# A second MLP's first layers in block products: seven products of half blocks in place of eight, with the sums of the weights made ahead

## Chip, core and metric

One core of one Trainium2 chip runs the whole program in one launch. The metric is the device time of the launch in microseconds, the median of several runs. TensorE is called PE here, VectorE DVE, ScalarE ACT, GpSimd POOL, and SyncE, whose queue issues the transfers, SP.

## The reference

Attention with its softmax on the queries (over the head's 64 numbers) and on the keys (over the sequence) gives 4608 tokens of 512 numbers. They go through two pairs of layers:

```python
# attention: q_s, k_s = softmaxes of q (last axis) and k (axis 2)
kv = np.einsum('bhsd,bhse->bhde', k_s, v)
x = np.einsum('bhsd,bhde->bhse', q_s, kv)      # 8 x 8 heads, 576 x 64
# then as 4608 x 512:
h = x @ w_in                                   # 512 x 2048
x = np.maximum(0.01 * h, h) @ w_out            # 2048 x 512
h = np.maximum(np.maximum(x @ w1, x @ w2), x @ w3)   # each 512 x 768
out = h @ w_out2                               # 768 x 512
```

All is float32 outside; the weights reach the chip as 64-bit words.

## The kernel before

The tokens stand in nine chunks of N = 512. Every operand of a product is kept as a high and a low part, and one product of blocks is three matmuls into one PSUM bank (`mm3`): high by high, high by low, low by high. A matmul has 128 rows, 128 columns of weights and 512 tokens. Two pools hold four banks each: `ps` for first layers, `ps_acc` (tile `acc`) for last layers.

The first pair (stage A) works through the chunks in the turns of the table TURNS, 16 steps of a block of 128 hidden numbers each. In a step PE makes the first layer's block (`project`, 12 matmuls), ACT takes it from the bank, ACT and DVE split it (`split_g`), and PE then makes the last layer's part of the step before (`a_out`, 12 matmuls). Beside it run units of background work, one stage per step: the attention of later chunks (`kv_unit`, `q_unit`) and, from step 33 on, the preparation of the second pair's weights. Each of 24 `ahead_unit`s loads 512 KB of raw words, splits them (`split_words`) into high and low parts in a buffer `room` of the pool `wp` and stores these to a DRAM tile `wb`. The results of stage A are stored to DRAM tiles `x2`.

In stage B the 12 prepared blocks of 1 MB (`weights_ready`, L170) stay in `wp`, which has 17 buffers of 1 MB. For each chunk and each of six m (MB = 6 blocks of 128 hidden numbers) three `project`s of 12 matmuls are made; ACT copies the first bank (L596), DVE takes the maximum with the second and the third (L597, L598), `split_g` makes the two parts, and PE makes the last layer's part of the m before (`b_out`, 12 matmuls). After the last m of a chunk ACT and DVE in turn copy four banks to `st` (L440, L438), and SP stores them (L441).

Each engine works its instructions off in its own order and waits for the others by semaphores. A scheduler puts the instructions of an engine in order when the program is built; the source decides it but for small shifts.

## Time and profile before

| | |
|---|---|
| runs | 1474.90, 1474.41, 1474.42 us; median 1474.42 |
| profiled execution (the span of its profile) | 1474.5 us |
| PE busy | 1455.5 us, 6984 matmuls |
| weight loads on PE | 1199.1 us, beside the matmuls |
| DVE busy | 730.3 us |
| ACT busy | 491.4 us |
| transfers | 129.24 MB |

Busy times are sums over instructions of the profiled execution. Matmuls follow each other before the one ahead has ended, so the mean length of one (390 ns) is more than the time from one to the next. Every DMA of the kernel is issued by SP.

### The profile page before, as it was taken

How to read it: one execution, taken by the hardware profiler on the slowest of the kernel's cores; microseconds unless marked ns; L12 is line 12 of the kernel's file. 1: busy time of each engine (PE TensorE's matmuls, PEld its weight loads, DVE VectorE, ACT ScalarE, POOL GpSimd, SP SyncE). 2: the span in 40 equal slices, each digit the busy share in tenths (PEclk: the TensorE clock that was granted, in tenths of full speed). 3: DMA queues.
4: the chain of work that ended last, by engine and by line, in shares of the span. 5: the costliest groups of instructions: out<-in, count | busy, mean ns of one | idle time of the engine just before them, and what ended most of it. 6: DMA issues, size and time to landing. Idle time of an engine off the chain costs nothing.

```text
span 1474.5 us, 17669 instructions
## 1 busy us (share of the span) xinstructions
PE 1455.5 (99%) x6984; PEld 1199.1 (81%) x6984; DVE 730.3 (50%) x1386; ACT 491.4 (33%) x968; POOL 28.6 (2%) x42
## 2 busy tenths in 40 slices
PE   7999999999999999999999999999999999999998
PEld 5688878888888888888888888888888888888887
DVE  9779955867666676765662162213122222222222
ACT  6755853444344344433432231212111111112111
POOL 0000100000000000000000000000000000000000
PEclk9999999999999999999999999999999999999999
DMA  9235532314232231412205580101010100000000
GB/s 356 85 116 185 205 98 72 107 62 130 72 125 78 85 129 62 129 57 68 93 30 186 199 338 33 58 1 58 0 58 3 56 29 29 29 0 29 1 29 29
DMA packets 45203, 129.24 MB, mean 88 GB/s; under 512 B 4672, under 2 KB 4672, under 8 KB 39488
## 3 DMA queue, kind: packets, MB, share of 16 engines
q1 hardware_dynamic: 45120, 128.11, 25.2%
q8 instruction: 55, 0.90, 0.3%
q14 instruction: 28, 0.23, 0.0%
HBM read 89.29 MB, written 38.80 MB: 87 GB/s over the span
## 4 chain that ended last, share of the span: by engine, by line
PE 96%; DVE 2%; ACT 1%; DMA 0%; issue 0%; SPq 0%; ACTq 0%
PE ps L410 56%; PE acc L410 37%; PE ps L377 1%; PE ps L258 1%; DMA spare<-in_q_dram 0%; DVE spare L344 0%; DVE nmx L224 0%; DVE qmx L325 0%; PE ps L359 0%; DVE spare L335 0%; DVE qsm L338 0%; DVE ca L130 0%; DVE raw L133 0%; DVE ca L134 0%; ACT spare L236 0%
## 5 line engine op out<-in xcount | busy, mean ns | idle before, releaser
L410 PE MATMUL ps<-xhi,w 128*128 128x512 f32 x2448 | 777.1, 390 | 1.9 <-DVE xlo L394 1.2
L410 PEld LDWEIGHTS ps<-xhi,w 128*128 128x128 f32 x2448 | 460.2, 188 | 98.6 <-DVE xlo L394 1.5
L410 PE MATMUL ps<-xlo,w 128*128 128x512 f32 x1224 | 476.6, 390 | 0.0
L410 PE MATMUL acc<-ghi,w 128*128 128x512 f32 x1152 | 381.9, 393 | 0.0
L410 PEld LDWEIGHTS ps<-xlo,w 128*128 128x128 f32 x1224 | 230.2, 188 | 48.2 <-ACT xlo L391 0.3
L410 PEld LDWEIGHTS acc<-ghi,w 128*128 128x128 f32 x1152 | 216.0, 188 | 46.6 <-ACT ghi L430 0.2
L431 DVE TENSOR_TENSOR glo<-g,ghi 128x512 fp32r<-128x512 f32 (+1 forms) x201 | 136.2, 679 | 227.7 <-ACT ghi L430 227.7
L410 PE MATMUL acc<-glo,w 128*128 128x512 f32 x576 | 224.5, 390 | 0.3 <-DVE glo L431 0.3
L430 ACT ACTIVATE ghi<-g 128x512 fp32r<-128x512 f32 (+1 forms) x201 | 125.2, 625 | 216.3 <-DVE g L598 208.8
L597 DVE TENSOR_TENSOR g<-g,ps 128x512 f32<-128x512 f32 x54 | 37.2, 688 | 306.1 <-PE ps L410 306.1
L552 ACT ACTIVATE g<-ps 128x512 f32<-128x512 f32 x144 | 85.5, 595 | 258.8 <-PE ps L410 255.5
L410 PE MATMUL acc<-w,ghi 128*128 128x512 f32 x432 | 132.8, 389 | 0.0
L410 PEld LDWEIGHTS acc<-glo,w 128*128 128x128 f32 x576 | 108.2, 188 | 22.3 <-DVE glo L431 0.5
L596 ACT ACTIVATE g<-ps 128x512 f32<-128x512 f32 x54 | 32.4, 599 | 201.1 <-PE ps L410 201.1
L410 PEld LDWEIGHTS acc<-w,ghi 128*128 128x128 f32 x432 | 81.0, 188 | 16.8
L598 DVE TENSOR_TENSOR g<-g,ps 128x512 f32<-128x512 f32 x54 | 37.2, 688 | 106.0 <-PE ps L410 106.0
L410 PE MATMUL acc<-w,glo 128*128 128x512 f32 x216 | 83.9, 389 | 0.0
L440 ACT ACTIVATE st<-acc 128x512 f32<-128x512 f32 x68 | 38.5, 599 | 60.4 <-PE acc L410 60.2
L410 PEld LDWEIGHTS acc<-w,glo 128*128 128x128 f32 x216 | 40.6, 188 | 8.5
L249 POOL PARTITION_ALL_REDUCE mx<-mx x24 | 25.5, 1063 | 629.2 <-DVE mx L248 619.1
L131 ACT ACTIVATE room<-ca 128x512 fp32r<-128x512 f32 x24 | 15.2, 633 | 56.0 <-DVE ca L130 56.0
L534 ACT ACTIVATE xhi<-xf 128x512 fp32r<-128x512 f32 x36 | 20.0, 623 | 36.9 <-PE ps L410 33.5
(110 smaller groups left out, 941.1 us busy)
## 6 DMA issues: line engine op xcount, KB each, us to landing
raw<-in_wa_dram SPq DMA_DIRECT2D x16, 1024.0 KB, 7.8
x<-st SPq DMA_DIRECT2D x64, 256.0 KB, 3.4
room<-in_wb_dram SPq DMA_DIRECT2D x24, 512.0 KB, 3.9
wb<-room SPq DMA_DIRECT2D x24, 512.0 KB, 3.0
w<-wb SPq DMA_DIRECT2D x12, 1024.0 KB, 5.1
xf<-x SPq DMA_DIRECT2D x9, 1024.0 KB, 4.9
out_dram<-st SPq DMA_DIRECT2D x36, 256.0 KB, 2.1
vt<-in_v_dram SPq DMA_DIRECT2D x24, 325.0 KB, 4.1
```

What stands on the lines that cost most here:

```text
L131: nc.scalar.activation(hi, af, AF.Copy)
L249: nc.gpsimd.partition_all_reduce(mx, mx, P, bass_isa.ReduceOp.max)
L258: nc.tensor.matmul(acc[z, : D + 1], lhsT=ke[:, r, z], rhs=vt[:, r, h], start=r == 0, stop=r == RK - 1)
L410: nc.tensor.matmul(acc, lhsT=l, rhs=r, start=first and i == 0, stop=last and i == 2)
L430: nc.scalar.activation(hi[:, z], g[:, z], AF.Copy)
L431: nc.vector.tensor_tensor(lo[:, z], g[:, z], hi[:, z].bitcast(F32), op=ALU.subtract)
L440: nc.scalar.activation(st, acc, AF.Copy)
L534: nc.scalar.activation(hi[:, kk], xf[:, kk], AF.Copy)
L552: nc.scalar.activation(g, acc, AF.Prelu, alpha=0.01)
L596: nc.scalar.activation(g, accs3[0], AF.Copy)
L597: nc.vector.tensor_tensor(g, g, accs3[1], op=ALU.max)
L598: nc.vector.tensor_tensor(g, g, accs3[2], op=ALU.max)
```

## The change

Chunk 0 of the second pair is computed as before. Chunks 1 to 8 are taken two by two. The tokens of a pair are put into two sides of 512 (the first halves of both chunks, the second halves), so that with the 512 inputs in two halves and two m's of weights at a time a product of 2 x 2 blocks arises. It is made by Strassen's seven block products in Winograd's form. A unit (t, j) is the pair of m's t and the first layer j; there are nine units in a pair of chunks, of seven products of six matmuls (L798). Of the weights' half blocks a11, a12 and a22 are operands themselves, and with a21 they make the four sums s1 to s4, which are the other four operands; the tokens' side has one operand to each of the seven (`operands`, named after the weights' operand that it meets).

A bank collects several products, and its sum on the way is read out by ACT (`snap`, L818) before the next product is added. `out` makes the four results of a unit from snapshots and banks (L829, L833: sums on DVE; L827: a copy on ACT) and keeps the maximum over j (L835). With j = 2 it makes the two parts of h (L842 on ACT, L843 on DVE). The last layers take the left side of tokens in `out_left` (24 matmuls for each t), the right side in `out_right` (18 for each block of 128 rows); they stand between s1 and s3 of some iterations as `fill`.

The sums of the weights are made in stage A by nine `ahead_unit`s, which store them to a DRAM tile `stream` in the order of use, and the plain halves to `plainw` for chunk 0. In the pair part they are loaded as groups of four products, 1 MB each, three groups ahead (`load_group`, 65 times). Tokens of a chunk are stored as two halves per piece throughout, so that the rows of the output go out by `store_rows`, 48 transfers in place of 36, copied from the bank by ACT alone.

```diff
+PAIRS = ((1, 2), (3, 4), (5, 6), (7, 8))
+H = N // 2
+USES = ("a11", "a12", "a22", "s2", "s4", "s1", "s3")
+LATE = ("a22", "s4")
+PARTS = ("a21", "a11", "a12", "a22", "s2", "s4", "s1", "s3")
...
-    ready = [[dp.tile([P, 2, 2, N], F32, name=f"wb{m}{i}") for i in range(2)] for m in range(MB)]
-
-    def ahead_unit(m, i, s):
...
+    UNITS = [(t, j) for t in range(MB // 2) for j in range(3)]
+    NU = len(UNITS)
+    CYCLE = len(USES) * NU
...
+        i = place(PARTS[at], u)
+        n = t.shape[1]
+        nc.sync.dma_start(stream[:, i : i + n, h], t)
+        if i < 3:
+            e = min(n, 3 - i)
+            nc.sync.dma_start(stream[:, CYCLE + i : CYCLE + i + e, h], t[:, :e])
...
+    def ahead_unit(u):
+
+        t, j = UNITS[u]
+        room = wp.tile([P, 4 * N], F32, tag="w", name="room")
+        b = room.rearrange("p (b n) -> p b n", n=H)
+        raw = room[:, 2 * N :].bitcast(wb.dtype)[:, :N]
+        for half in range(2):
+            nc.sync.dma_start(raw, wb[2 * t + half, j // 2, :, j % 2])
+            yield
+            yield
+            split_words(raw, None, None, N, after=newest["g"], whole=b[:, 1:3] if half == 0 else b[:, 0:4:3])
+        yield
+        a21, a11, a12, a22, s2, s4, s1, s3 = (b[:, i] for i in range(8))
+        nc.vector.tensor_tensor(s1, a21, a22, op=ALU.add)
+        nc.vector.tensor_tensor(s2, s1, a11, op=ALU.subtract)
+        nc.vector.tensor_tensor(s3, a11, a21, op=ALU.subtract)
+        nc.vector.tensor_tensor(s4, a12, s2, op=ALU.subtract)
+        for first in (4, 0):
+            yield
+            hi = cp.tile([P, 2 * N], F32R, tag="ca", name="hi")
+            z = room[:, first * H : first * H + 2 * N]
+            nc.scalar.activation(hi, z, AF.Copy)
+            nc.vector.tensor_tensor(z.bitcast(F32R), z, hi.bitcast(F32), op=ALU.subtract)
+            for h, t in enumerate((hi.bitcast(F32).rearrange("p (b n) -> p b n", n=H), b[:, first : first + 4])):
+                if first:
+                    for at, n in ((0, 1), (1, 1), (2, 2)):
+                        to_stream(u, t[:, at : at + n], 4 + at, h)
+                else:
+                    nc.sync.dma_start(plainw[u][:, :, h], t)
+                    for at, n in ((1, 2), (3, 1)):
+                        to_stream(u, t[:, at : at + n], at, h)
+
+    def ahead_out(m):
...
     def ahead_units():
-        first = 2 * MA + 1
-        for j in range(4 * MB):
-            yield first + 4 * j, ahead_unit(j // 4, j // 2 % 2, j % 2)
...
+        at = 2 * MA + 1
+        for u in range(NU):
+            yield at, ahead_unit(u)
+            at += 8
...
+    def store_rows(i, c, col, acc):
+
+        st = gp.tile([P, N], F32, tag="st", name="st", bufs=4)
+        nc.scalar.activation(st, acc, AF.Copy)
+        at = 0
...
+    def load_group(g):
+
...
+        w = wp.tile([P, 4, 2, H], F32R, tag="w", name="group")
+        at = 4 * g % CYCLE
+        n = min(4, total - 4 * g)
+        ins = nc.sync.dma_start(w[:, :n].bitcast(F32), stream[:, at : at + n])
+        tc.keep_in_program_order(ins)
+        groups[g] = w
+
...
+    def part(at):
+        g = at // 4
+        while len(groups) <= min(g + AHEAD, (len(PAIRS) * CYCLE + LAST - 1) // 4):
+            load_group(len(groups))
+        return groups[g][:, at % 4]
...
+    def operands(sides, ops):
+
+        b11, b21 = sides[0][:, :2], sides[0][:, 2:]
+        b12, b22 = sides[1][:, :2], sides[1][:, 2:]
+
...
+            o = ops[name] = operand()
+            for kk in range(2):
+                nc.scalar.activation(o[:, 0, kk], t[:, kk], AF.Copy)
+                nc.vector.tensor_tensor(o[:, 1, kk], t[:, kk], o[:, 0, kk].bitcast(F32), op=ALU.subtract)
+
...
+    def product(bank, name, at, ops, fresh):
+        w = part(at)
+        for kk in range(2):
+            z = slice(kk * P, kk * P + P)
+            a = (w[:, 0, z], w[:, 1, z])
+            b = tuple(ops[name][:, h, kk] for h in range(2))
+            for i, (l, r) in enumerate(((a[0], b[0]), (a[0], b[1]), (a[1], b[0]))):
+                first, last = kk == i == 0, kk == 1 and i == 2
+                nc.tensor.matmul(
+                    bank, lhsT=l, rhs=r, start=fresh and first, stop=last, skip_group_check=not fresh
+                )
...
+        def snap(self, bank):
+            t = bp[0].tile([P, N], F32, tag="snap", name="snap", bufs=5)
+            nc.scalar.activation(t, bank, AF.Copy)
+            return t
+
...
+        def out(self, i, bank, snap=None):
+
+            if self.j == 0:
+                tag, bufs = (("g", 2), ("ghi", 2), ("glo", 2), ("st", 4))[i]
...
+                if snap is None:
+                    nc.scalar.activation(g, bank, AF.Copy)
+                else:
+                    nc.vector.tensor_tensor(g, snap, bank, op=ALU.add)
+                return
+            g = self.best[i]
...
+            if snap is not None:
+                nc.vector.tensor_tensor(snap, snap, bank, op=ALU.add)
+                bank = snap
+            nc.vector.tensor_tensor(g, g, bank, op=ALU.max)
+            if self.j == 2:
+                side, m = i % 2, i // 2
...
+    def iteration(new, *fill):
+
+        nonlocal old
+        if new is not None:
+            new.a, c = psum(), psum()
+            new.product(new.a, "a11", fresh=True)
+            first = new.snap(new.a)
+            new.product(c, "a12", fresh=True)
+            new.out(0, c, first)
+        if old is not None:
+            old.product(old.a, "a22")
+            old.out(2, old.a)
+        if new is not None:
+            new.product(new.a, "s2")
+            new.s = new.snap(new.a)
+        if old is not None:
+            old.product(old.b, "s4")
+            old.out(1, old.b, old.s)
+        if new is not None:
+            new.b = psum()
+            new.product(new.b, "s1", fresh=True)
+        for f in fill:
+            f()
+        if new is not None:
+            new.product(new.a, "s3")
+            new.out(3, new.b, new.snap(new.a))
+        old = new
+
...
+    def out_left(p, t):
+
...
+        for r in range(4):
+            for m in (2 * t, 2 * t + 1):
+                mm3(accs[p, 0][r], h_of(p, m, 0, r), wo(m), m == 0, m == MB - 1)
...
-            accs3 = [project(wB[m][j], cur) for j in range(3)]
-            g = f32_tile()
-            nc.scalar.activation(g, accs3[0], AF.Copy)
...
+    for p in range(len(PAIRS)):
+        nxt, building = {}, iter(())
+        for u in range(NU):
+            if u % 3 == 0:
+                best = {}
...
+            if u == 0:
+                fill = [lambda a=prev: b_out(*a)] if p == 0 else [lambda q=p - 1: out_left(q, 2)]
+            if u in (1, 2) and p > 0:
+                fill = [lambda q=p - 1, r=r: out_right(q, r) for r in (2 * u - 2, 2 * u - 1)]
+            if u in (3, 6):
+                fill = [lambda q=p, t=u // 3 - 1: out_left(q, t)]
...
+                if u == 4:
+                    building = operands(sides, nxt)
+                for _ in range(1 if u < NU - 1 else 99):
+                    next(building, None)
```

The first place is PE at the beginning of the pair part. Before, this is one m: the end of the third `project` into its bank, the last layer's 12 matmuls into four `acc`, and the next m.

```order
L410 MATMUL ps_8354<-xlo_7864,w_7514 128x512
L410 MATMUL ps_8354<-xhi_7863,w_7514 128x512
L410 MATMUL acc_8182<-w_7426,ghi_8312 128x512 x2
L410 MATMUL acc_8182<-w_7426,glo_8313 128x512
L410 MATMUL acc_8183<-w_7426,ghi_8312 128x512 x2
L410 MATMUL acc_8183<-w_7426,glo_8313 128x512
L410 MATMUL acc_8184<-w_7426,ghi_8312 128x512 x2
L410 MATMUL acc_8184<-w_7426,glo_8313 128x512
L410 MATMUL acc_8185<-w_7426,ghi_8312 128x512 x2
L410 MATMUL acc_8185<-w_7426,glo_8313 128x512
L410 MATMUL ps_8387<-xhi_7863,w_7547 128x512
L410 MATMUL ps_8387<-xlo_7864,w_7547 128x512
```

After, behind the last matmuls of chunk 0, come the second unit's a11 and a12 (operands op_8020 and op_8025), around them s3 and a22 of the first unit (op_8231, op_8236, both into ps_8246), and then s2 (op_8160), s4 (op_8241) and s1 (op_8167) of the one or the other.

```order
L498 MATMUL acc_7942<-wB_7734,ghi_8215 128x512
L498 MATMUL acc_7942<-wB_7734,glo_8216 128x512
L798 MATMUL ps_8317<-op_8020,group_8097 128x512 x6
L798 MATMUL ps_8318<-op_8025,group_8099 128x512 x6
L798 MATMUL ps_8246<-op_8231,group_8097 128x512 x6
L798 MATMUL ps_8246<-op_8236,group_8099 128x512 x6
L798 MATMUL ps_8317<-op_8160,group_8099 128x512 x6
L798 MATMUL ps_8274<-op_8241,group_8099 128x512 x6
L798 MATMUL ps_8361<-op_8167,group_8248 128x512 x6
L798 MATMUL ps_8380<-op_8020,group_8248 128x512 x6
L798 MATMUL ps_8317<-op_8231,group_8248 128x512 x6
L798 MATMUL ps_8381<-op_8025,group_8248 128x512 x6
```

Six matmuls of a product now stand together, and a bank is added to again after others were: ps_8317 by s2 and later by s3. In the first unit a22 stands directly behind s3 of the same bank, ps_8246. In the second unit a12 (op_8025, bank ps_8381) stands between s3 (op_8231, bank ps_8317) and what follows on that bank.

Still in the pair part, this is ACT, which reads the banks. Before, one m has a copy of a bank to `g` and the split into `ghi`, and at a chunk's end two copies of `acc`.

```order
L430 ACTIVATE ghi_10661<-g_10657 128x512
L596 ACTIVATE g_10716<-ps_10677 128x512
L430 ACTIVATE ghi_10720<-g_10716 128x512
L596 ACTIVATE g_10775<-ps_10736 128x512
L440 ACTIVATE st_10786<-acc_10474 128x512
L430 ACTIVATE ghi_10779<-g_10775 128x512
L440 ACTIVATE st_10798<-acc_10476 128x512
L596 ACTIVATE g_10846<-ps_10807 128x512
```

After, in the second pair of chunks, the reads of one unit's bank (ps_9660: after a11, s2 and s3) stand among the copies of h and the splits of the next pair's tokens (`op` from `side`).

```order
L818 ACTIVATE snap_9654<-ps_9595 128x512
L818 ACTIVATE snap_9668<-ps_9660 128x512
L763 ACTIVATE op_9728<-side_9262 128x512 x2
L818 ACTIVATE snap_9696<-ps_9660 128x512
L842 ACTIVATE h0_9680<-best0_9519 128x512
L763 ACTIVATE op_9740<-side_9263 128x512 x2
L763 ACTIVATE op_9735<-side_9262 128x512 x2
L818 ACTIVATE snap_9721<-ps_9660 128x512
L818 ACTIVATE snap_9763<-ps_9755 128x512
```

Between the reads of s2 (snap_9696) and of s3 (snap_9721) there are five other operations here.

The second place is PE at the end of the program. Before, the last m's 12 matmuls of the last layer follow those of the m before.

```order
L410 MATMUL acc_10856<-w_7514,glo_11032 128x512
L410 MATMUL acc_10857<-w_7514,ghi_11031 128x512 x2
L410 MATMUL acc_10857<-w_7514,glo_11032 128x512
L410 MATMUL acc_10854<-w_7596,ghi_11090 128x512 x2
L410 MATMUL acc_10855<-w_7596,ghi_11090 128x512 x2
L410 MATMUL acc_10854<-w_7596,glo_11091 128x512
L410 MATMUL acc_10856<-w_7596,ghi_11090 128x512 x2
L410 MATMUL acc_10855<-w_7596,glo_11091 128x512
L410 MATMUL acc_10857<-w_7596,ghi_11090 128x512 x2
L410 MATMUL acc_10856<-w_7596,glo_11091 128x512
L410 MATMUL acc_10857<-w_7596,glo_11091 128x512
```

After, a22 and s4 of the last unit are followed by the left side's last layer (acc_10946 to acc_10949), and then come the right side's blocks, 18 matmuls each; between s3 and this a22 stand four matmuls.

```order
L798 MATMUL ps_11268<-op_10559,group_11223 128x512 x6
L798 MATMUL ps_11312<-op_10564,group_11256 128x512 x6
L498 MATMUL acc_10946<-wB_7734,h0_11286 128x512 x2
L498 MATMUL acc_10947<-wB_7734,h0_11286 128x512 x2
L498 MATMUL acc_10948<-wB_7734,h0_11286 128x512 x2
L498 MATMUL acc_10949<-wB_7734,h0_11286 128x512 x2
L498 MATMUL acc_10946<-wB_7734,h0_11286 128x512
L498 MATMUL acc_10947<-wB_7734,h0_11286 128x512
L498 MATMUL acc_10948<-wB_7734,h0_11286 128x512
L498 MATMUL acc_10949<-wB_7734,h0_11286 128x512
L498 MATMUL acc_11388<-wB_7437,h1_10889 128x512 x6
L498 MATMUL acc_11388<-wB_7570,h1_11112 128x512 x6
```

The last unit's h (h0_11286, h1_11329) is needed one product after a22, and the first right block takes a bank of `ps_acc` anew.

The third is SP in stage A, at the preparation of the weights. Before, each unit is one load and one store.

```order
L305 DMA qt_6753<-in_q_dram 128x512
L166 DMA wb50_149<-room_6485 256x1x512
L162 DMA room_6664<-in_wb_dram 128x512
L166 DMA wb50_149<-room_6664 256x1x512
L162 DMA room_6837<-in_wb_dram 128x512
L166 DMA wb51_150<-room_6837 256x1x512
```

After, a unit has two loads into one `room`, and stores of the high parts (`hi`, one buffer for both of a unit) and the low parts (`room`).

```order
L212 DMA room_6611<-in_wb_dram 128x512
L200 DMA stream_139<-hi_6874 128x256 x2
L200 DMA stream_139<-hi_6874 128x2x256
L200 DMA stream_139<-room_6611 128x256 x2
L200 DMA stream_139<-room_6611 128x2x256
L233 DMA plainw8_148<-hi_6918 512x1x256
L200 DMA stream_139<-hi_6918 128x2x256
L200 DMA stream_139<-hi_6918 128x256
L203 DMA stream_139<-hi_6918 128x256
L233 DMA plainw8_148<-room_6611 512x1x256
```

The stores of hi_6874 stand ahead of hi_6918's, which is written to the same buffer.

## Rows read from the trace of the kernel before

**Rows 1.** Parts 1, 2 (40 slices) and 4 of the page.

```profile
PE 1455.5 (99%) x6984; PEld 1199.1 (81%) x6984; DVE 730.3 (50%) x1386; ACT 491.4 (33%) x968; POOL 28.6 (2%) x42
...
PE   7999999999999999999999999999999999999998
...
DVE  9779955867666676765662162213122222222222
...
PEclk9999999999999999999999999999999999999999
...
PE 96%; DVE 2%; ACT 1%; DMA 0%; issue 0%; SPq 0%; ACTq 0%
PE ps L410 56%; PE acc L410 37%; PE ps L377 1%; PE ps L258 1%; DMA spare<-in_q_dram 0%; DVE spare L344 0%; DVE nmx L224 0%; DVE qmx L325 0%; PE ps L359 0%; DVE spare L335 0%; DVE qsm L338 0%; DVE ca L130 0%; DVE raw L133 0%; DVE ca L134 0%; ACT spare L236 0%
```

**Rows 2.** Chain in order of time: start us, length us, engine, tile, line.

```profile
977.87 8.16 PE ps L410 x36
...
1456.58 8.16 PE ps L410 x36
```

**Rows 3.** Windows: stretch, length, busy us (x), clock, DMA share, GB/s.

```profile
20.00:24.00 4.00, 2.72 (x82) 2.47 (x81) 4.00 (x8) 2.22 (x6) 0.00 (x0) 1.00 1.04 390
...
52.00:56.00 4.00, 2.06 (x7) 1.56 (x8) 3.88 (x7) 2.59 (x7) 0.00 (x0) 0.96 0.00 0
56.00:60.00 4.00, 4.00 (x12) 3.06 (x12) 2.64 (x4) 1.22 (x3) 0.00 (x0) 0.62 0.01 4
...
400.00:600.00 200.00, 200.00 (x1049) 166.54 (x1047) 136.13 (x305) 83.71 (x167) 8.11 (x8) 1.00 0.30 99
845.00:884.00 39.00, 39.00 (x174) 32.30 (x173) 26.53 (x43) 13.09 (x23) 0.00 (x0) 1.00 0.82 325
...
960.00:1090.56 130.56, 130.56 (x577) 108.11 (x576) 32.19 (x48) 21.13 (x36) 0.00 (x0) 1.00 0.09 33
```

**Rows 4.** Timeline of the end: start us, length us, instruction, [idle before].

```profile
1464.78 0.69 DVE L598 TENSOR_TENSOR g<-g,ps 128x512 f32<-128x512 f32 x1 [1.96 <-PE ps L410]
...
1465.50 0.91 ACT L430 ACTIVATE ghi<-g 128x128 fp32r<-128x128 f32 x4 [5.50 <-DVE g L598]
...
1469.57 0.61 PE L410 MATMUL acc<-w,glo 128*128 128x512 f32 x2
...
1470.22 0.69 DVE L438 COPY st<-acc 128x512 f32<-128x512 f32 x1 [0.21 <-PE acc L410]
```

**Rows 5.** Page, part 5: copies from banks, maxima and splits.

```profile
L431 DVE TENSOR_TENSOR glo<-g,ghi 128x512 fp32r<-128x512 f32 (+1 forms) x201 | 136.2, 679 | 227.7 <-ACT ghi L430 227.7
...
L430 ACT ACTIVATE ghi<-g 128x512 fp32r<-128x512 f32 (+1 forms) x201 | 125.2, 625 | 216.3 <-DVE g L598 208.8
L597 DVE TENSOR_TENSOR g<-g,ps 128x512 f32<-128x512 f32 x54 | 37.2, 688 | 306.1 <-PE ps L410 306.1
...
L596 ACT ACTIVATE g<-ps 128x512 f32<-128x512 f32 x54 | 32.4, 599 | 201.1 <-PE ps L410 201.1
```

**Rows 6.** Timeline at 52 us, the attention's products.

```profile
52.12 0.58 ACT L383 ACTIVATE xhi<-ps 128x512 fp32r<-128x512 f32 x1
...
52.75 0.47 PE L388 MATMUL ps<-xhi,kvhi 128*128 128x448 f32 x1 [0.83 <-ACT xhi L383]
```

**Rows 7.** Groups by line and shape: the split of prepared weights.

```profile
L135 DVE TENSOR_TENSOR w<-ca,raw 128x1024 fp32r<-128x1024 f32 x16 | 19.5, 1220 | 0.2
...
L131 ACT ACTIVATE w<-ca 128x1024 fp32r<-128x1024 f32 x16 | 17.0, 1064 | 15.2 <-DVE ca L130 15.2
...
L135 DVE TENSOR_TENSOR room<-ca,room 128x512 fp32r<-128x512 f32 x24 | 16.6, 691 | 0.8
```

**Rows 8.** Loads of line L170 (1 MB each): time to landing.

```profile
DMA to landing us min/median/max: 4.7/5.1/11.5
```

**Rows 9.** Stores of line L166 (512 KB each): SP's time, time to landing.

```profile
L166 SPq DMA_DIRECT2D wb<-room x24: 524/525/603, 261.5 to 796.5; - x24
...
DMA to landing us min/median/max: 3.0/3.0/5.2
```

More of the change, by code (lines that the diff above doesn't have):

```diff
@@ new lines, in part, with raw_pair @@
+    def part(at):
[3 more added lines that the diff above has]
+        return groups[g][:, at % 4]
+    def raw_pair(pair):
+        sides = [wp.tile([P, KDM, N], F32, tag="w", name="side") for _ in range(2)]
+        more = []
+        for i, c in enumerate(pair):
+            mine = [turn for turn in turns if turn[0] == c]
+            for s in range(2):
+                z = slice(s * H, s * H + H)
+                nc.sync.dma_start(sides[s][:, :, i * H : i * H + H], x2[mine[0]][:, :, z])
+            for turn in mine[1:]:
+                t = wp.tile([P, KDM, N], F32, tag="w", name="part")
+                nc.sync.dma_start(t, x2[turn])
+                more.append((i, t))
+        return sides, more
@@ new lines, in tile_kernel @@
+    for m in range(MB):
+        accs3 = [project_b(m, j, cur) for j in range(3)]
+        g = f32_tile()
+        nc.scalar.activation(g, accs3[0], AF.Copy)
+        nc.vector.tensor_tensor(g, g, accs3[1], op=ALU.max)
+        nc.vector.tensor_tensor(g, g, accs3[2], op=ALU.max)
+        hpair = split_g(g)
+        if m == 0:
+            a_out(*prev)
+            sides, more = raw_pair(PAIRS[0])
+        else:
+            b_out(*prev)
+        if m == 1:
+            add_parts(sides, more)
+            ops = {}
+            building = operands(sides, ops)
+        if m >= 2:
+            for _ in range(2 if m < MB - 1 else 99):
+                next(building, None)
+        if m == 3:
+            for i in range(AHEAD):
+                load_group(i)
+        prev = (0, m, hpair)
@@ L615 @@
+    iteration(None)
+    out_left(len(PAIRS) - 1, 2)
+    for r in range(4):
+        out_right(len(PAIRS) - 1, r)
 _OUTS = [((4608, 512), "float32")]
```

224 lines of the change are left out of this document (165 added, 59 removed).

## The prediction

> **What bounds the kernel now.** I read the busy shares first: PE is busy for 1455.5 of 1474.5 us, DVE for half of the span and ACT for a third [rows 1]. The 40 slices say where: PE is at 9 in all but the first, and its clock line too, so that almost the whole span is matmuls at the higher of the two clock levels (2.4 GHz); DVE is loaded in the first half and at 1 to 3 tenths in the second, where the second pair of layers runs [rows 1]. The chain that ended last is 96% PE, nearly all of it on the helper line L410 [rows 1]. The third view is that chain in order of time: in the second pair each group of 36 matmuls into `ps` starts 10.88 us after the last one, 44 times from 977.87 to 1456.58 [rows 2]. One such step is one m of one chunk: 36 matmuls of the three first layers and 12 of the last layer. So one matmul takes 10.88 / 48 = 0.22667 us of PE time, and the second pair consists of nothing else. The span is 0.08 us above the median of the runs, so what is taken from one holds for the other.
>
> **What is removed.** In before two chunks take 2 x 6 x 48 = 576 matmuls. After, a pair of chunks takes nine units of 7 products x 6 matmuls, 378, and the same 144 of the last layer, 522. That is 54 fewer per pair and 216 for the four pairs; the lengths (128x512) are the same. At the pace above a pair goes from 130.56 us to 118.32, and all four save 216 x 0.22667 = 48.96 us. The windows check the pace: 577 matmuls in the 130.56 us of one pair of chunks (0.2263), 174 in 39.00 (0.2241) while the transfer engines are 82% busy [rows 3]; by the lowest of these the saving is 48.4. Chunk 0 and all of the first pair of layers keep their number of matmuls. The accumulation onto a bank that was already read is a matmul like those that continue a sum now, and I give it the same price.
>
> The Trainium skill, "TensorE: Matmul & The Clock Gate", section "Wait — 56ns, not 53.3ns?", gives 215.7 ns from start to start for 512 columns at the full clock. By it the saving would be 46.6 us. The chain's 226.67 ns decides here, since it is this kernel's own matmul.
>
> **What the snapshots add on PE's path.** The running sum of a bank is read (L818, on ACT) between two products that add to it. A wait there has three legs. From the end of a matmul's slot to the reader's start 0.20 us: the last two matmuls start at 1469.57, so their slots end 0.45 us later at 1470.02, and the copy starts at 1470.22 [rows 4]. The read on ACT 0.60 [rows 5]. From ACT's end to the next matmul 0.05: `xhi` ends at 52.12 + 0.58 = 52.70, the matmul starts at 52.75 [rows 6]. Together 0.85 us. In the order most reads have ten or more matmuls of other banks behind them (2.27 us); at 17 places, those between s3 and a22 of a unit with nothing to fill in, there are six, 1.36 us. That covers 0.85 with 0.51 left, so I cost the steady pattern at nothing; without the six matmuls each place would cost 0.85. In the first unit there is no previous unit, and s3 and a22 stand directly behind each other: 0.85 us. At the end a22 has four matmuls ahead of it (0.91, enough). The left operand of the last layer then goes PE 0.20, max on DVE 0.69, DVE to ACT 0.03 (1464.78 + 0.69 = 1465.47, and ACT starts at 1465.50 [rows 4]), ACT 0.60, 0.05: 1.57 us against the six matmuls of s4, 0.21 late. The first right block needs the bank whose copy stands behind the last h1 on ACT: I put about 0.64 there from the same legs: that h1 comes after DVE's subtraction for h0, a sum and a maximum of 0.69 each, and the bank's last matmul has long been done. The tail gives back 0.85, and gets 0.09 from a last copy by ACT (0.60) in place of DVE (0.69) [rows 4, 5].
>
> **DVE and ACT in the pair part.** DVE gets 340 operations of 128x512 in the four pairs, 85 per pair: 36 sums of a snapshot and a bank for j = 0, 72 and 96 for the others (sum, then max), 48 subtractions for h, and 88 for the operands. At 0.69 [rows 5] that is 58.7 us of the 118.3. Before, the same stretch has 32 of 130.56 [rows 3]. ACT gets 256 operations of 0.60 to 0.63, 39 us per pair. Neither fills its time; in the first half DVE works at 136 of 200 us with PE at 200.00 [rows 3], so such a load beside PE is seen. A sum of an SBUF tile and a bank isn't in the trace; the max of the same two, L597, is, at 688 ns, which I take. Its bounds are 0.60 (ACT's copy of a bank) and 1.22 (twice the width, [rows 7]). At 1.22 a pair would take 104 us on DVE, still below 118.
>
> **The weights made ahead.** 24 loads of the prepared second-pair weights become 18 raw halves, nine units of four sums, and six of the old kind. Per raw half DVE loses one 0.69 operation [rows 7] and ACT one of 0.63 [rows 5]; per unit DVE gets two of 128x1024 at 1.22, ACT two at 1.06 [rows 7]. The 36 sums of 128x256 are not in the trace; between 0.2 and the 0.69 of double the width I take 0.43, from 1.22 - 0.69 = 0.53 for 512 more columns. DVE: -12.4 + 22.0 + 15.5 = +25 us, ACT: -11.4 + 19.1 = +8. They fall into about 500 us in which DVE has a third free. PE stays covered as long as ACT's own order does, for ACT reads PE's banks there (rival 2).
>
> **The stream.** 65 loads of 1 MB, each for four products, so one per 7.3 us of the pair part's 4 x 118.3 = 473. A 1 MB load lands in 5.1 us in the middle, 11.5 at most [rows 8]. Each is issued at least 85 matmuls, 19.3 us, before its first use, and when its buffer comes free. 68 MB over 473 us are 144 GB/s; PE had its pace under 325 [rows 3]. Nothing on the path. The 48 stores of output rows in place of 36 are short and behind copies.
>
> **The sum.** 1474.5 - 48.96 + 0.85 + 0.85 - 0.09 = 1427.2 us, a gain of 47.3.
>
> **Rivals.** *1. The read is late.* At the 17 places ACT has one or two other operations (a copy of h, a split of an operand, 0.62 each) beside the snapshot. One of them just ahead makes the read 0.62 - 0.51 = 0.11 late, two make it 0.73. Over 17 places that is 1.9 to 12.4 us: 1429.1 to 1439.6. For it: these operations wait for DVE, which is now at half load, and so their times wander. Against it: in the order they stand between the reads of s2 and of s3, 24 matmuls or 5.44 us apart, and are five at most, 3.1 us. 0.13.
> *2. Stage A waits for its small stores.* The second `hi` of a unit takes the one buffer that the stores of the first must have left; they are issued right behind it. With 1.06 for the first `hi` [rows 7], 1.6 for three issues of 0.525 and 3.2 for a landing like that of `wb` [rows 9] this is 5.9 us, against 24 matmuls or 5.44 between the two: ACT is late by 0.4. PE has 5.44 - 0.60 - 0.63 - 0.68 = 3.5 in hand: the next project and last-layer part are 24 matmuls, and the copy and the split of a step take the rest [rows 5]. If these stores take the 11.5 us that the slowest `wb` store took [rows 9], PE loses 14.2 - 5.44 - 3.5 = 5.2 us; at three of nine units this is 16, 1443, at all nine 47, which takes the gain away. What is behind the wait is ACT's reading of `ps`, and behind that PE. 0.05.
> *3. The clock falls: slower.* Seven short products with a wait between them are a new pattern. Between 52 and 56 us PE was busy for 2.06 of 4 us, and in the next 4 us the granted clock was 0.62 and 12 matmuls ran, where 17.6 fit: 1.3 us lost per fall [rows 3]. From 47.3 / 1.3 = 36 falls on, one per unit, nothing is left; at 1.5 per unit it is 54 x 1.3 = 70 us, 1497. Against it: with 2.72 of 4 us busy, 20 to 24 us, the clock stayed at 1.00 [rows 3], and a stall of 0.85 us per unit would leave PE over 90% busy. 0.03. The same page of the Trainium skill, section "A second HAM failure mode: psum-queue depth-cycling", says that a kernel which cycles through its PSUM banks can idle briefly between groups of matmuls so often that the clock swings; the row at 20 us does not bear it out at this load.
> *4. The stream is late.* From 47.3 / 65 = 0.73 us per group the gain is gone. It needs loads below 130 GB/s, or SP held by an output store that waits for ACT. The lead of 19.3 us speaks against it; at half of that, 1450. 0.02.
>
> **How the numbers follow.** The sum holds with 0.76, and its own range is 1425.4 (nothing given back) to 1431 (three times the waits named). Together with rival 1 this is 0.89, and I take 1424.5 to 1438, the lower end from the 0.5 us by which the pace is known and from stalls of the start that could shift. A measurement here tells 0.2%, 2.9 us, from no change. Faster: the sum, rivals 1 and 2, and half of 4: 0.95. Slower: rival 3 and a little of 4: 0.035. Within 0.2%: what is left, 0.015.
>
> **What would show it.** PE with 6768 matmuls and about 19 to 21 us of idle time in all; a pair in 118.3 us; the clock line at 9. Rival 1 would show as waits of PE for the L818 reads, beyond two, mostly of 0.1 to 0.7 us; rival 2 as PE idle between 230 and 800 us, behind ACT; rival 3 as a clock below 1.00 in the pair part; rival 4 as waits of PE for `group`. I am wrong if PE's time per matmul in the pair part isn't 0.2267 with the clock at 1.00, for which no row gives a reason, or if PE waits for DVE, whose operations I have priced by their like.

## The result and the profile after

The changed kernel takes 1428.48 us (median of 4 runs, 1427.44 to 1429.37) against 1474.41: 45.9 us less, ratio 0.9684, 95% interval 0.967 to 0.9698. The forecast was 1427.2 in a range of 1424.5 to 1438.

The page of the changed kernel, parts 1, 2, 4 and the snapshots' group of part 5:

```profile
PE 1408.2 (99%) x6768; PEld 1159.7 (81%) x6768; DVE 835.5 (59%) x1559; ACT 558.5 (39%) x1079; POOL 27.6 (2%) x42
...
DVE  9778964877766676667664225524463462463242
...
PEclk9999999999999999999999999999999999999999
...
PE acc L498 38%; PE ps L498 31%; PE ps L798 24%; PE ps L466 1%; PE ps L346 1%; DVE spare L433 0%; DMA spare<-in_q_dram 0%; DVE nmx L312 0%; DVE qmx L414 0%; PE ps L447 0%; DVE spare L424 0%; DVE qsm L427 0%; DVE ca L154 0%; DVE raw L158 0%; DVE ca L163 0%
...
L818 ACT ACTIVATE snap<-ps 128x512 f32<-128x512 f32 x108 | 61.7, 597 | 143.8 <-PE ps L798 143.1
```

PE has the 216 matmuls less and 17.8 us of idle time (19.0 before). DVE goes from 50% to 59% and ACT from 33% to 39% [rows 1], most of it in the second half, and the clock line stays at 9. A snapshot takes 0.60 us, as the copies of before do [rows 5].

The chain of the changed kernel in order of time (columns as in [rows 2]):

```profile
890.11 8.16 PE ps L498 x36
...
1023.01 20.40 PE ps L798 x90
...
1141.34 20.40 PE ps L798 x90
...
1259.65 20.40 PE ps L798 x90
```

Its windows of the first pair of layers and of three pairs of chunks (columns as in [rows 3]):

```profile
200.00:400.00 200.00, 199.31 (x1025) 164.22 (x1024) 132.82 (x292) 85.41 (x167) 8.22 (x9) 1.00 0.37 118
400.00:600.00 200.00, 200.00 (x1049) 166.66 (x1048) 141.23 (x317) 84.60 (x166) 7.15 (x8) 1.00 0.39 126
600.00:800.00 200.00, 200.00 (x939) 166.01 (x938) 125.24 (x270) 78.17 (x145) 2.72 (x3) 1.00 0.33 107
...
1000.00:1118.30 118.30, 118.30 (x524) 98.00 (x523) 55.01 (x85) 36.80 (x65) 0.00 (x0) 1.00 0.49 178
1118.30:1236.60 118.30, 118.30 (x524) 98.01 (x522) 54.99 (x85) 36.55 (x65) 0.00 (x0) 1.00 0.48 174
1236.60:1354.90 118.30, 118.30 (x523) 98.02 (x522) 51.39 (x79) 35.35 (x63) 0.00 (x0) 1.00 0.49 182
```

The same product of a pair starts 118.33 and 118.31 us after that of the pair before: 522 matmuls at 0.2267, PE busy for all of it at a clock of 1.00. The first pair of layers is untouched: PE 199.31 of 200 and 200.00 of 200.

PE's waits, all that last 0.7 us or more in sum:

```profile
PE t L307 <- DMA spare<-in_k_dram: 4.7, 3, 3.8
PE t L307 <- ACT spare L326: 1.4, 1, 1.4
PE ps L478 <- ACT xhi L472: 1.3, 2, 0.8
PE ps L498 <- DVE xlo L482: 1.2, 1, 1.2
PE ps L346 <- ACT plain L354: 0.9, 2, 0.5
PE ps L798 <- ACT snap L818: 0.7, 1, 0.7
PE ps L447 <- ACT qf L441: 0.7, 1, 0.7
PE ps L498 <- ACT g L644: 0.7, 1, 0.7
```

One line of it belongs to the pair part: a single wait for a snapshot. There is none for `group`. (The list goes by the ends of matmuls as the profile shows them, which lie 0.16 us behind the end of a slot, 0.39 in place of 0.2267; so two short waits at the end of the last pair are not in it.) The timeline at that wait:

```profile
953.64 3.11 PE L798 MATMUL ps<-op,group 128*128 128x512 f32 x13
...
956.79 1.09 ACT L818 ACTIVATE snap<-ps 128x512 f32<-128x512 f32 x2 [3.44 <-PE ps L798]
...
957.44 2.79 PE L798 MATMUL ps<-op,group 128*128 128x512 f32 x11 [0.69 <-ACT snap L818]
```

And the last copy in the timeline:

```profile
1422.37 0.60 ACT L676 ACTIVATE st<-acc 128x512 f32<-128x512 f32 x1 [3.48 <-PE acc L498]
```

The 13 matmuls from 953.64 fill 2.95 us, to 956.59; the read starts at 956.79, and the next matmul at 957.44, 0.85 later, as the three legs had it. The matmuls behind the wait then take 0.13 longer: 11 of them show 2.79 where 10 x 0.2267 + 0.39 = 2.66 would be.

Executions differ in their first 60 us, so I measure from one m of chunk 0 (890.11 in the chain above) to the beginning of the last copy. In the chain of before the same m is:

```profile
890.83 8.16 PE ps L410 x36
```

It is the second m of chunk 0, and the last copy starts at 1470.22 [rows 4]: 579.39 us. After, it is 1422.37 - 890.11 = 532.26, which is 47.13 less. The sum of the terms that lie in this stretch is 48.96 - 0.85 - 0.85 = 47.26. From the last copy to the end of the span it takes 4.28 before and 3.63 after.

### The profile page after: what moved, and what is told of

Its sections match the earlier page's. It is cut to its first block, busy times and chain, and to the rows that moved or that the text cites. A ratio compares the mean times of both kernels' runs of the same rounds, so it can differ in the third digit from the quotient of the medians.

```text
span 1426.0 us, 17847 instructions
## 1 busy us (share of the span) xinstructions
PE 1408.2 (99%) x6768; PEld 1159.7 (81%) x6768; DVE 835.5 (59%) x1559; ACT 558.5 (39%) x1079; POOL 27.6 (2%) x42
## 4 chain that ended last, share of the span: by engine, by line
PE 96%; DVE 2%; ACT 1%; DMA 0%; issue 0%; SPq 0%; ACTq 0%
PE acc L498 38%; PE ps L498 31%; PE ps L798 24%; PE ps L466 1%; PE ps L346 1%; DVE spare L433 0%; DMA spare<-in_q_dram 0%; DVE nmx L312 0%; DVE qmx L414 0%; PE ps L447 0%; DVE spare L424 0%; DVE qsm L427 0%; DVE ca L154 0%; DVE raw L158 0%; DVE ca L163 0%
## 5 line engine op out<-in xcount | busy, mean ns | idle before, releaser
L498 PE MATMUL ps<-xhi,w 128*128 128x512 f32 x1152 | 371.0, 391 | 1.9 <-DVE xlo L482 1.2
L798 PE MATMUL ps<-op,group 128*128 128x512 f32 x1512 | 352.9, 390 | 0.7 <-ACT snap L818 0.7
L798 PEld LDWEIGHTS ps<-op,group 128*128 128x128 f32 x1512 | 283.8, 188 | 60.0 <-ACT snap L818 1.3
L498 PEld LDWEIGHTS ps<-xhi,w 128*128 128x128 f32 x1152 | 217.1, 188 | 48.0 <-DVE xlo L482 1.5
L498 PE MATMUL ps<-xlo,w 128*128 128x512 f32 x576 | 224.8, 391 | 0.0
L519 DVE TENSOR_TENSOR glo<-g,ghi 128x512 fp32r<-128x512 f32 x150 | 103.2, 688 | 195.6 <-ACT ghi L518 195.3
L498 PE MATMUL acc<-wB,h 128*128 128x512 f32 x576 | 140.4, 390 | 0.1
L498 PEld LDWEIGHTS ps<-xlo,w 128*128 128x128 f32 x576 | 108.5, 188 | 22.8 <-ACT xlo L479 0.3
L498 PEld LDWEIGHTS acc<-wB,h 128*128 128x128 f32 x576 | 108.0, 188 | 23.2 <-ACT h L842 0.5
L833 DVE TENSOR_TENSOR snap<-snap,ps 128x512 f32<-128x512 f32 x72 | 49.4, 687 | 119.0 <-ACT snap L818 92.4
L818 ACT ACTIVATE snap<-ps 128x512 f32<-128x512 f32 x108 | 61.7, 597 | 143.8 <-PE ps L798 143.1
L518 ACT ACTIVATE ghi<-g 128x512 fp32r<-128x512 f32 x150 | 94.6, 631 | 23.2 <-DVE g L904 18.1
L829 DVE TENSOR_TENSOR best<-snap,ps 128x512 f32<-128x512 f32 x36 | 24.7, 687 | 93.6 <-PE ps L798 43.7
L842 ACT ACTIVATE h<-best 128x512 fp32r<-128x512 f32 x48 | 30.3, 632 | 95.6 <-DVE best L835 95.3
L835 DVE TENSOR_TENSOR best<-best,snap 128x512 f32<-128x512 f32 x72 | 49.2, 690 | 1.6
```

What stands on the lines that cost most here:

```text
L498: nc.tensor.matmul(acc, lhsT=l, rhs=r, start=first and i == 0, stop=last and i == 2)
L518: nc.scalar.activation(hi[:, z], g[:, z], AF.Copy)
L519: nc.vector.tensor_tensor(lo[:, z], g[:, z], hi[:, z].bitcast(F32), op=ALU.subtract)
L798: nc.tensor.matmul(bank, lhsT=l, rhs=r, start=fresh and first, stop=last, skip_group_check=not fresh)
L818: nc.scalar.activation(t, bank, AF.Copy)
L829: nc.vector.tensor_tensor(g, snap, bank, op=ALU.add)
```

## Experiments

The theory under test: PE's matmuls alone set the time; a read of a bank costs nothing with six or more matmuls beside it and 0.85 us without. Rivals: reads, DVE, the stream or the clock take a share that is small here by chance. In what follows "the stretch" is that from chunk 0's second m to the last copy, read from each profile; it is 532.26 in the changed kernel. Spans and times also hold the start.

**The kernel before, again** (no edit).

> The kernel before once more, for its span beside its time. The changed kernel's time is 1.8 us longer than the span of the same execution. Theory (that is the same for every program, and the 0.1 us between the span and the median of before was two different executions): 1.8 us here too, a span of 1472.6 beside 1474.4. Rival (the changed kernel has something outside its span that before hasn't): at most 0.5 us here.

Its profiled execution took 1474.93 us and has a span of 1473.2: 1.7 us lie outside the span, as with the changed kernel's 1427.8 and 1426.0. So the span of 1474.5 belonged to an execution of about 1476.2, 1.8 above the median of 1474.42; the kernel before took 1474.0 to 1477.1 in the runs of this study. The stretch is 1468.81 - 889.42 = 579.39, the same to 0.01, and the start is 1.41 earlier.

**The changed kernel, again** (no edit).

> The changed kernel once more, beside the next run on the same chip. Its times stand in two groups, 1427.4 to 1427.8 and 1429.2 to 1429.4, as those of before do (1474.2 to 1475 and 1476 to 1476.8). Theory (the two groups come from the first 60 us, where the clock falls once or twice, and the rest is the same in every execution): the profile has 532.3 us from chunk 0's second m to the last copy's beginning, whatever its start. Rival (the pair part itself varies): that stretch differs by more than 0.3 us.

Median 1428.64 (1426.97 to 1428.68). The stretch is 1423.25 - 890.99 = 532.26, again the same to 0.01. So these two executions differ in the start only.

**An eighth product per unit.**

```diff
             new.product(new.b, "s1", fresh=True)
+            new.product(new.b, "s1", fresh=True)
```

> The product of s1 is made twice in each of the 36 units (the second pass starts its bank anew), so that a unit has eight products again, with all snapshots, sums and streams of seven. Theory (PE's matmuls alone set the time, everything else is hidden): 216 matmuls x 0.2267 us = +49.0 us over the changed kernel's 1428.5, 1477.5, with PE's idle time as it is. Rival (PE is held up by ACT's and DVE's reads, which would now get 1.36 us more per unit): less than +40 us, below 1468.

1480.87 us, ratio to before 1.004 (1.0025 to 1.0055); the stretch is 585.34, 53.1 more. 48.96 of it is the added matmuls. The rest, 4.1, is of the new order: the scheduler set fewer matmuls beside some reads. From PE's waits in this run (us in all, times, longest):

```profile
PE ps L798 <- ACT snap L818: 2.6, 9, 0.7
```

The list names 0.69 of the 0.98 that the first unit's wait costs, 0.29 too little; with that, nine waits are 2.6 + 9 x 0.29 = 5.2 us, 4.2 more than the changed kernel's one. Eight of the nine last 0.24 on average in the list and 0.40 behind the end of the slot: by estimate that is 0.85 less two matmuls of 0.2267, so two stood beside each of these reads. The structure with snapshots, sums and stream is thus worth nothing without the smaller count of matmuls, and the count is paid in full.

**PE's order pinned to the source.** a22 stands 12 matmuls behind s3.

```diff
+    pinned.append(True)
     for p in range(len(PAIRS)):
...
-                nc.tensor.matmul(
+                ins = nc.tensor.matmul(
...
+                tc.keep_in_program_order(ins)
```

> PE's order in the pair part is pinned to that of the source: a22 stands 12 matmuls behind s3 everywhere, in the first unit too, but directly behind it in the last. Theory: the 0.7 us of the first unit goes and as much comes at the end, 1428.5 within 1 us, and PE has no wait for a snapshot but the last. Rival (at the 17 places with six matmuls the read is now and then late): 2 to 12 us less, 1416 to 1426.

1431.41 us (1428.82 to 1432.37); the stretch is 534.21, 1.95 more. The first unit's wait is gone and the last unit's has come. What I hadn't expected is a third: at the boundary of the first two pairs PE waits for h, where the last layer's matmuls now stand in one block (at this place of the changed kernel the scheduler had put 2 to 8 at a time between the products). The other two boundaries have such a block and no such wait; why was not tried. From PE's waits in this run:

```profile
PE acc L500 <- DVE h L848: 2.1, 2, 1.9
...
PE ps L802 <- ACT snap L823: 0.7, 1, 0.7
```

The pairs behind it repeat in 118.32 us as in the changed kernel, so the 17 places with six matmuls had cost nothing: no gain of 2 to 12 us.

**No matmul beside the read after s3**, in the pinned order.

```diff
-        if old is not None:
-            old.product(old.a, "a22")
-            old.out(2, old.a)
...
             new.out(3, new.b, new.snap(new.a))
+            new.product(new.a, "a22")
+            new.out(2, new.a)
```

> PE's order in the pair part is pinned, and a22 of a unit stands directly behind s3 on the same bank, so that the read between them has no matmul beside it, 36 times in place of once. Theory (one uncovered read costs its three legs): by the sum's 0.85 us 36 x 0.85 - 0.7 = +30 us, 1458; by the 0.7 us that the first unit of the changed kernel waited +24.5, 1453. PE shows 36 waits for the snapshot. Rival (reads cost PE something whatever stands beside them): the same +0 to +10 as now, below 1439. Rival on the clock: with a wait in every unit the granted clock falls below 1.00 in the pair part, and it costs 60 us or more, above 1488.

1463.19 us; the stretch is 568.73, 34.5 more than with the pinned order alone: 35 uncovered reads more, 0.99 each on average. PE's list has 39 waits for the snapshot where 36 were expected, three of them at the boundaries, and the wait for h there is shorter than in the pinned run (0.3 us in place of 2.1), so the average isn't the price of one read alone; a single unit gives that. One unit with its read at the end and the next one's first matmuls, and the windows of 400 us and of one unit:

```profile
1256.78 9.81 PE L802 MATMUL ps<-op,group 128*128 128x512 f32 x42 [0.69 <-ACT snap L823]
...
1266.63 0.60 ACT L823 ACTIVATE snap<-ps 128x512 f32<-128x512 f32 x1 [2.96 <-PE ps L802]
...
1267.28 0.96 PE L802 MATMUL ps<-op,group 128*128 128x512 f32 x3 [0.69 <-ACT snap L823]
```

```profile
1000.00:1400.00 400.00, 378.56 (x1631) 303.46 (x1630) 171.29 (x263) 114.94 (x198) 0.00 (x0) 1.00 0.44 159
1246.28:1256.78 10.50, 9.81 (x42) 7.81 (x42) 2.76 (x5) 2.39 (x4) 0.00 (x0) 1.00 0.41 147
```

42 matmuls fill 9.52 us, and the next unit starts 10.50 after this one: 0.85 of waiting and 0.13 at the restart. The direction is the theory's, and the price is 0.98 in place of 0.85. A wait in every unit doesn't take the clock down: 1.00, with PE busy for 378.56 of 400.

**The read after s3 four times**, pinned.

```diff
-            nc.scalar.activation(t, bank, AF.Copy)
+            for _ in range(times):
+                nc.scalar.activation(t, bank, AF.Copy)
...
-            new.out(3, new.b, new.snap(new.a))
+            new.out(3, new.b, new.snap(new.a, 4))
```

> Pinned order as in the run before, and the bank is read four times after s3 in place of once (the same copy). In ACT's order two of these reads stand ahead of the next unit's a11 read and two behind it, so that at 33 places PE waits: from the end of a11 0.20 + 3 x 0.60 + 0.05 = 2.05 us against the 1.36 of a12. Theory (legs of 0.20, 0.60 and 0.05): 33 x 0.69 + about 4 for the last unit and the three pair boundaries = +27 us, 1455; with legs as short as the first unit's wait of 0.7 (0.15 less) 33 x 0.54 + 3 = +21, 1449. Rival (more work on ACT is only load, the reads come in time anyway): +0 to +3, below 1432.

1464.7 us; the stretch is 569.96, 35.8 more than pinned alone. The usual unit behaves as counted; two that follow each other, in the chain of this run:

```profile
1248.45 8.47 PE ps L802 x36
1258.71 8.47 PE ps L802 x36
```

It takes 10.26 us, 0.74 over 9.52 (0.69 was counted). The other 11 us, for which I had allowed 4, are the units at the boundaries, where ACT's splits of the next pair's tokens (`op` from `side`) stand among the reads, and the last one, which waits for 2.6 us and behind which the granted clock is 0.79 between 1432 and 1440 us. So the read isn't free by itself; it was free because of what stood beside it.

**A rearranged end**, pinned: last-layer matmuls stand ahead of and behind a22 and s4 of the last unit, and the last right blocks use banks of `ps`.

```diff
-    iteration(None)
-    out_left(len(PAIRS) - 1, 2)
+    left(MB - 2, (0, 1))
+    old.product(old.a, "a22")
+    old.out(2, old.a)
+    old.product(old.b, "s4")
+    old.out(1, old.b, old.s)
+    left(MB - 2, (2, 3))
+    left(MB - 1, range(4))
```

> Pinned order; six matmuls of the last layer stand between s3 and a22 of the last unit, eighteen behind s4, and the last right blocks take banks of the other pool, so that no read in the pair part stands without cover. Theory: the first unit's 0.98 (0.85 of waiting and 0.13 in which the first matmul behind a wait starts later) and 0.9 at the end go, 1.9 us less than the changed kernel: 1426.6 median, and PE has no wait behind the first 60 us but the one after the attention's. Rival (the ends are hidden in the last copy and store anyway): 1428.5. The start varies by more than that from execution to execution, so the pair part is to be read from the profile: its four pairs, each 118.32 us, and the stretch from the last pair's beginning to the last matmul.

1427.1 us (1426.8 to 1429.63). The stretch is 532.67: 1.54 less than pinned, 0.4 more than the changed kernel, since the wait for h at the first boundary is still there. The expected 1.9 wasn't reached for that reason.

**The ends alone**: pinned in the first two units and from the last one on, with the same end.

```diff
+            pinned[:] = [True] * (p == 0 and u < 2 or p == len(PAIRS) - 1 and u == NU - 1)
             iteration(Unit(p, u, ops, best), *fill)
```

> The changed kernel with the order pinned only in the first two units (a22 twelve matmuls behind s3) and from the last unit on, with the end rearranged as in the run of that name; the steady part is left to the scheduler, so that the wait for h at the first pair's boundary, which came with the pinned order, isn't there. Theory: 0.98 at the first unit and 0.85 at the end go: 530.4 us from chunk 0's second m to the last copy in place of 532.3, and the median 1.8 us below the changed kernel's on this chip, if the starts are alike. Rival (as with the fully pinned order, another wait takes their place): 532 or more.

Median 1426.89 (1424.38 to 1427.26), ratio 0.9669 (0.9656 to 0.9682), beside 1428.64 for the changed kernel on the same chip. The stretch is 530.49 (530.4 was expected), 1.77 less; PE's waits show none for a snapshot or for h. Of all runs it has the shortest stretch. By the medians alone it can't be told from the changed kernel, whose interval overlaps; the stretch tells it.

**Maxima repeated**, on the rearranged end.

```diff
-            nc.vector.tensor_tensor(g, g, bank, op=ALU.max)
+            for _ in range(3):
+                nc.vector.tensor_tensor(g, g, bank, op=ALU.max)
```

> As the run before, with each maximum over j made three times (the same result), 192 more DVE operations of 0.69: DVE at 92 of 118 us per pair. Theory (DVE's load is hidden while the order leaves 12 matmuls beside each read): +0 to +3 over the run before, all of it at the end of the last pair, whose h is two maxima later. Rival (DVE at half load was near the bound already): PE waits for DVE in every unit, +10 or more.

1463.6 us; the stretch is 566.73, 34.1 more. My theory of 0 to 3 is wrong, and the rival is wrong in its place: the waits are not in every unit. Two windows at a boundary of pairs, of this run (columns as in [rows 3]):

```profile
1172.00:1180.00 8.00, 3.75 (x13) 2.48 (x12) 8.00 (x15) 2.98 (x7) 0.00 (x0) 0.88 0.00 0
1180.00:1188.00 8.00, 8.00 (x26) 6.30 (x26) 7.28 (x13) 3.65 (x8) 0.00 (x0) 0.69 0.38 132
```

At this boundary DVE is busy without a break, PE loses 4.25 of the 8 us, and behind that the granted clock is 0.69 on average: for part of the window it stands at the lower of its two levels (1.2 and 2.4 GHz). Each of the three boundaries has one long wait for a maximum (us in all, times, longest):

```profile
PE ps L802 <- DVE best L841: 10.0, 3, 3.7
```

To see whether this starts at once, the same with each maximum twice:

> The run with three maxima again, with two: 24 more DVE operations per pair of chunks (16.6 us), 75 of 118. With three it cost 34 us, nearly all at the three boundaries and the end of the last pair, where DVE was busy for 8.00 of 8 us. Theory (DVE is full there already, since the next pair's operands are built in the last units, so what is added there is paid at once, while the rest of the pair hides it): 2 to 4 us per boundary, +6 to +14 over the run with one, and no wait elsewhere. Rival (only the average load counts, and 75 of 118 is hidden): +0 to +2. Other rival (linear in the added operations): +17.

1442.69 us; the stretch is 546.68, 14.0 more, at the upper end of the range and short of the linear 17. Windows of 8 us of this run, those around the boundaries in which PE lost time:

```profile
1048.00:1056.00 8.00, 3.56 (x15) 2.31 (x13) 8.00 (x15) 4.91 (x10) 0.00 (x0) 0.97 0.26 107
1056.00:1064.00 8.00, 7.27 (x20) 5.79 (x21) 1.27 (x3) 1.79 (x3) 0.00 (x0) 0.60 0.21 68
...
1176.00:1184.00 8.00, 6.46 (x28) 4.71 (x27) 8.00 (x14) 5.41 (x10) 0.00 (x0) 1.00 0.13 38
...
1296.00:1304.00 8.00, 5.55 (x18) 3.68 (x17) 8.00 (x14) 3.39 (x6) 0.00 (x0) 0.83 0.19 81
```

In three of the four DVE is at 8.00 of 8; PE's loss is at the boundaries and at the last pair's end, and nowhere else. Not all of it is waiting for DVE. PE's waits for h in this run:

```profile
PE acc L500 <- ACT h L848: 6.0, 3, 3.0
PE acc L500 <- DVE h L849: 3.0, 3, 2.2
```

The run with the rearranged end has 1.9 us of them. By estimate from the windows the lower clock behind the waits takes another (1 - 0.60) x 8 + (1 - 0.83) x 8 = 4.6 of the 14.0 us. So the waits alone are inside the range of 6 to 14, and the clock, which the theory left out, brings the total to its end.

The changed kernel itself is busy on DVE at the same place. Its windows at the first boundary:

```profile
1036.00:1044.00 8.00, 8.00 (x37) 6.64 (x36) 8.00 (x14) 4.03 (x7) 0.00 (x0) 1.00 0.00 0
1048.00:1052.00 4.00, 4.00 (x19) 3.32 (x18) 4.00 (x7) 2.40 (x5) 0.00 (x0) 1.00 0.73 262
```

DVE has no free time for 8 us, and PE still loses nothing. Both runs with repeated maxima have the pinned order, in which PE waited for h at the first boundary already; how much more DVE work the changed kernel's own order would bear was not tried.

**One group ahead in place of three**, on the rearranged end.

```diff
-AHEAD = 3
+AHEAD = 1
```

> As the run with the rearranged end, with the stream loaded one group ahead in place of three. By the order nine loads have a lead of 25 to 37 matmuls (5.7 to 8.4 us) and all others 61 or more (13.8 us). A group landed in 6.4 us in the middle and 14.4 at most. Theory (only the lead against the landing counts): at some of those nine places PE waits for the group, 1 to 4 us each, +3 to +20 in all, and nowhere else. Rival (the stream is held by bandwidth, whatever the lead): waits at most of the 65 groups, +40 or more. Other rival (the landing is shorter with fewer loads on their way): +0 to +2.

1449.58 and 1454.32 us; the stretch is 554.81, 22.1 more. PE's wait for the stream in this run, and the window of the longest:

```profile
PE ps L802 <- DMA group<-stream: 12.9, 5, 6.0
```

```profile
1100.00:1108.00 8.00, 3.42 (x8) 2.78 (x9) 4.19 (x7) 1.15 (x2) 0.00 (x0) 0.61 1.03 421
```

Five waits for `group`, 12.9 us; bandwidth doesn't hold the other 60. By the trace these five loads were issued 2.8 to 6.4 us before PE needed them, later than the order's shortest lead of 5.7 to 8.4 would have it, and landed in 5.0 to 8.8. In the window of the longest wait the transfer engines are busy throughout (1.03, 421 GB/s), so that there the loads beside it may have a part too. The total is above my range, since I had left out what a long wait draws after it: other waits, and a clock of 0.61 around the longest. With three ahead a group lands in 2.7, 6.4 and at most 14.4 us after its issue, with a lead of 19.3 us or more, and PE waits for none.

## Why the prediction was right

**The count of matmuls** carried it: 48.96 us at the pace that [rows 2] gave, of which 47.13 are left. 522 matmuls in 118.32 us are again 226.67 ns each; an estimate with the 215.7 ns of the Trainium skill ("TensorE: Matmul & The Clock Gate", section "Wait — 56ns, not 53.3ns?") is 112.6 us per pair, and the trace does not agree for these matmuls.

**The uncovered reads.** The first unit's term was 0.85 and costs 0.98, the wait as predicted and 0.13 that the matmuls behind a wait take longer, a leg that the sum left out. The rest of the difference, 48.96 - 47.13 - 0.98 = 0.85, is the tail, and its total is the predicted one. Its parts are not. From the timeline of the changed kernel, a22 and s4 of the last unit, and from its chain, the last layer behind them:

```profile
1399.57 2.97 PE L798 MATMUL ps<-op,group 128*128 128x512 f32 x12
```

```profile
1402.62 3.01 PE acc L498 x12
1405.67 16.63 PE acc L498 x72
```

The slots of the first twelve end at 1399.57 + 12 x 0.2267 = 1402.29, 0.33 before the left operand's matmuls start (0.21 was forecast); these fill 2.72, and the first right block starts 0.33 behind them, 0.13 of it the restart (0.64 was forecast); its own restart adds another 0.13. That these parts come so near to the forecast 0.85 is luck. Both terms are confirmed by taking them away together: 1.77 us in the run with the ends alone rearranged. Rival 1 didn't occur; not one of the 17 places waited.

**The end.** 0.09 was forecast for the last copy, 0.65 came. The rest is behind the copy: in before the last two copies start 0.23 us apart and their stores go out together, after the last two copies are 4.08 us apart. The last store lands 2.4 us after its issue in before and 2.0 after, which is most of the difference. That the stores beside it are the cause wasn't tried.

**Span and median.** "The span is 0.08 us above the median of the runs, so what is taken from one holds for the other" was a step that failed: a time lies 1.7 to 1.8 above the span of its own execution, in both kernels, and the two numbers came from different executions. That it did no harm is luck: the profiled execution had one of the longer starts, and so its span fell on the median of the others. The 1.3 us between forecast and median are not of the pair part. From the last copy on and in the stretch 47.8 us went; the rest is the start, which differs by 2 us between executions of either kernel: the four runs of before lay at 1474.35 to 1474.9, the four of the changed kernel at 1427.4 to 1427.8 and at 1429.2 to 1429.4. What makes the start differ was not tried, but the profiles show a part of it. The first 38 matmuls behind the first chunk's attention, in the chain of the changed kernel and in that of the run with the ends alone:

```profile
53.86 10.39 PE ps L498 x38
```

```profile
53.67 8.91 PE ps L500 x38
```

In the changed kernel the granted clock is 0.85 from 48 to 56 us and 0.94 from 56 to 64, in the other run 1.00 in both. Over the 13 profiles these matmuls take 10.34 to 10.55 us in the seven in which the clock fell there, and 8.89 to 8.93 in the other six: about 1.5 us. Why it falls in one execution and not in the next stays open. The start is also part of the reason why PE's idle time is 17.8 us and not the 19 to 21 that were named as a sign: PE was busy for 59.41 of the first 72 us, and for 58.02 in before.

**Stage A.** PE was not touched, and rival 2's wait is there, larger than I put it: ACT waits 16.0 us in nine units for the stores, 1.8 each in place of 0.4. From the view of that line (L226) in the changed kernel, what ended ACT's idle time before it (us, times):

```profile
  DMA stream<-hi: 16.0, 9
```

The 3.5 us in hand covered it. The stores land in 1.7, 2.7 and at most 5.1 us. The prices of this rival were misread: [rows 9] has 3.0 us in the middle and 5.2 at most for a `wb` store, where the prediction says 3.2 and 11.5; the 11.5 is the slowest load of [rows 8]. By the 5.2 ACT would have been 1.06 + 1.6 + 5.2 - 5.44 = 2.4 late, inside the 3.5, so that these rows gave no reason for a loss.

**DVE's bound** was a wrong argument for a right result. I said that at 1.22 per operation a pair would take 104 us on DVE, "still below 118", and so safe. The runs with repeated maxima cost 14 us at 75 and 34 us at 92 us per pair: the load is hidden unit by unit, not over a pair, and in the last two units, where the next operands are made, DVE is full. I named such a wait in the last sentence only and gave it no chance of its own. What kept it away was the scheduler's order, whose last-layer matmuls stand between the products at the boundary: with them in one block (the pinned order) PE waited 1.9 us for h, and the prediction hadn't counted on that.

**The clock.** It stayed at 1.00, as forecast. A wait of 0.85 in each unit leaves it there too, so rival 3's price per fall had no occasion. The Trainium skill's section "A second HAM failure mode: psum-queue depth-cycling" of the same page isn't borne out by banks that cycle with waits of this size. In the pair part the clock fell only in the runs with repeated maxima, with one group ahead and, at the last unit, with four reads (0.79 from 1432 to 1440 us, behind 8 us in which PE was busy for 5.58).

**A small slip.** The prediction says that PE's row in [rows 1] is at 9 in all but the first slice; the last one is at 8.

## What to carry to other kernels

When PE sets the time, fewer matmuls pay in full, if every read of a bank has other matmuls beside it; count them in the order as it was built, and allow a restart for each that has none. A share of busy time over a long stretch doesn't show that an engine has room: look at the few microseconds where its work is densest. Compare a span with the time of the same execution, and a stretch between two fixed instructions with itself: it repeats to 0.01 us where the times spread over 2.

## What the runs showed of the hardware

The matmuls behind a wait cost 0.13 us more than the wait (0.98 per uncovered read where the legs add up to 0.85). The granted clock stayed at 1.00 with a wait of 0.85 us in every 10.5, and was 0.60 and 0.69 in the 8 us behind windows in which PE was busy for 3.56 and 3.75 of 8. 1.7 to 1.8 us of an execution lie outside its span, in every profiled one whose time is on record.
